# Five softmax normalisations of the first two token chunks on VectorE instead of GpSimd, one PSUM copy on ScalarE, and a new hand-written order

## The chip, the cores and the metric

The kernel runs on one core of one Trainium2 chip. The metric is the device time of one execution in microseconds (us). Engines are TensorE (PE in the profile; PEld are its weight loads), VectorE (DVE), ScalarE (ACT), GpSimd (POOL) and SyncE (SP), which issues the DMAs. Every engine runs its own queue in order; between queues the order is kept by semaphores.

## The reference

Sliding-window attention (window 64) over 8 batches, 8 heads, 576 positions and a head size of 64, followed by a two-layer network with a rational function between its layers. q, k, v and the output are float32; the two weight matrices arrive as float64.

```python
scores = (q @ k.T) / sqrt(64)                    # per batch and head
scores = where((rel >= 0) & (rel < 64), scores, -1e9)
attn = exp(scores - max(scores));  attn = attn / (sum(attn) + 1e-9)
x = (attn @ v) as [4608 tokens, 512]             # heads side by side
h = x @ w_in                                     # [4608, 2048]
P = a0 + a1*h + a2*h**2 + a3*h**3
Q = 1 + |b0|*|h| + |b1|*h**2
out = (P / (Q + 1e-6)) @ w_out                   # [4608, 512]
```

## The kernel before

**Work.** The 4608 tokens go in nine chunks c of 512. Each chunk has four *units* (c,hp), one for each pair of heads: SP loads q, k and v; TensorE makes the scores (L641; for the first two chunks a matmul with the mask, L624, comes first); VectorE takes the row maxima (L679, L680); ScalarE makes the exponentials and their sums (L691); VectorE inverts the sums (L698, L699); then *normalise* multiplies the probabilities `sm`, 128 x 1024, by the inverse (L703, on GpSimd); TensorE transposes them into two PSUM banks (L708); *copy_pT* brings them to SBUF (L716); TensorE multiplies by v into `ps_x` (*values*, L722); *x_high* rounds that to fp32r (L727) and *x_low* keeps the rest (L731, VectorE).

For each chunk there are then 16 steps over slices of 128 of the 2048 columns, 144 steps s in all. A step has *G* s (12 matmuls, L802: high and low parts of x and w_in), its rational function (ScalarE L808, L811, L814, L827, L830; VectorE L817 num1, L820 num2, L834 g_high, L838 product, L842 remainder, L847 g_low; GpSimd L824 u1) and *F* s.0 to s.3, one for each 128 tokens (3 matmuls each, L885, into four PSUM accumulators). Chunk 0 does its first 8 steps, then chunk 1 all 16, then chunk 0 the rest, and the other chunks follow.

The float64 weights come as 32 *tiles* of bits, W0i to W15i for w_in and W0o to W15o for w_out, and are taken apart once, within about the first 200 us: SP loads a tile (L501, L503), ScalarE scales its high words (L507 *scale*), GpSimd keeps the sign (L511 *sign*), VectorE joins the bits (L515 *put_sign*, L520 *put_low*), ScalarE makes the high part (L531 *high*) and VectorE the low one (L534 *rest*).

**PSUM.** `h` and `ps_x` share two buffers: a G or a unit's values wait until num2 or x_low has read the buffer's last owner. The scores of chunk 1 and all transposes share the two banks `b0` and `b1`.

**Order.** All of these operations go into a plan. A list scheduler gives each a start, but for the first 200 us a table `PLACE` (operation number to start) overrides it. The operations are emitted in the order of these starts, which sets the order of each engine's queue and nothing else; SP's DMAs wait for the buffer that they fill and block the DMAs behind them.

```python
for op in self.ops:
    op.start = PLACE.get(op.n, op.start)
return sorted(self.ops, key=lambda o: o.start)
```

Loads of w_st tiles stand in staging buffers of several pools: W0o and W4i, and the probabilities of unit (0,1), share the two `sm` buffers.

Of the kernel before, what the change touches and what calls it, by code (L numbers as in the profile page):

```python
# [13 lines left out]
ALU = mybir.AluOpType  # L14
# [31 lines left out]
class Plan:  # L46
# [25 lines left out]
    def order(self):  # L72
# [92 lines left out]
        for op in self.ops:  # L165
# [5 lines left out]
PLACE = {0: 8.17349, 1: 38.92356, 2: -5.9611, 3: 8.88229, 4: 1.33916, 5: 1.47189, 6: 3.78178, 7: 8.4872, 8: 9.67491,  # L171
# [123 lines left out]
def swa_rational_ffn(ctx: ExitStack, tc: tile.TileContext, qT, kT, v, w_in, w_out, a, b, out):  # L295
    nc = tc.nc
    P = 128
# [85 lines left out]
    wi_h, wi_l, wo_h, wo_l = {}, {}, {}, {}  # L383
# [36 lines left out]
    UN, GT, F2R, OUTR, N1, SG, LD = 0.3, 0.02, 0.5, -0.5, 0.0, 0, 2.0  # L420
    KEEP = 4
    PT_DVE = ((0, 0), (0, 1))
    XH_DVE = ((0, 0), (0, 1))
    LENT = ((0, 1),)
    MASK_US = 4.8
    PSC = 8
# [134 lines left out]
    def plan_unit(c, hp, rank):  # L561
# [12 lines left out]
        u = {}  # L574
# [415 lines left out]
```

## Time and profile before

| | |
|---|---|
| median of 3 runs | 956.92 us (956.54 to 958.22) |
| profiled execution, time | 956.61 us |
| profiled execution, span of instructions | 954.8 us |
| TensorE busy | 934.4 us, 98% of the span |
| VectorE busy | 789.6 us, 83% |
| ScalarE busy | 670.4 us, 70% |
| GpSimd busy | 331.0 us, 35% |
| mean granted clock of TensorE | 0.993 |

The busy shares are means over stages: a long steady stage of steps, and the first 200 us or so, in which weights are decoded too. The difference of 1.8 us between the profiled execution's time and its span lies around the instructions. In rows of the timeline the square bracket tells how long the engine idled before an instruction and what ended that.

### The profile page before, as it was taken

To read this page: it belongs to the slowest core of one execution; us is meant where nothing else is said; L and a number is where in the kernel's file an instruction comes from. 1 tells how busy PE (TensorE), PEld (TensorE's weight loads), DVE (VectorE), ACT (ScalarE), POOL (GpSimd) and SP (SyncE) were. 2 spreads that over 40 slices of the span, in tenths; PEclk is the share of its full clock that TensorE was granted. 3 is DMA by queue.
4 is the path that set the end of the run, shared out by engine and by line. 5 is a ranking of instruction groups with operands and counts; after the bars stand their busy time and mean duration, and the time that the engine had idled before them with its cause. 6 is when DMAs were issued, how large, how long until landed. Compare 5 with 4: busy or idle time off the path is not lost.

```text
span 954.8 us, 16307 instructions
## 1 busy us (share of the span) xinstructions
PE 934.4 (98%) x6068; PEld 751.6 (79%) x6068; DVE 789.6 (83%) x1198; ACT 670.4 (70%) x1477; POOL 331.0 (35%) x227
## 2 busy tenths in 40 slices
PE   7789999999999999999999999999999999999998
PEld 5567777878888888888888888888888888888886
DVE  5999999999797978887787787878879778777775
ACT  6787877778767676666767677667676676756564
POOL 5756456433423233232323233233132332322221
PEclk9899999999999999999999999999999999999999
DMA  8732315123421112101111121111211120001001
GB/s 317 244 133 65 131 46 154 46 92 104 136 82 44 44 44 87 44 13 58 61 44 44 43 81 50 45 48 48 92 46 46 46 83 31 1 1 45 0 1 45
DMA packets 39103, 66.47 MB, mean 70 GB/s; under 512 B 5616, under 2 KB 22256, under 8 KB 39024
## 3 DMA queue, kind: packets, MB, share of 16 engines
q1 hardware_dynamic: 39024, 65.43, 20.7%
q8 instruction: 48, 0.79, 0.3%
q14 instruction: 31, 0.25, 0.1%
HBM read 54.92 MB, written 10.49 MB: 69 GB/s over the span
## 4 chain that ended last, share of the span: by engine, by line
PE 88%; DVE 8%; ACT 2%; issue 1%; DMA 0%; POOL 0%; SPq 0%; ACTq 0%; DVEq 0%; POOLq 0%
PE o L885 39%; PE h L802 39%; PE ps_x L722 3%; PE banks L641 3%; PE banks L708 2%; ACT sm L691 1%; DVE gh L834 1%; DVE num L842 1%; DVE nmx L679 1%; DVE num L817 1%; DVE u L838 1%; DVE w_c L515 1%; DVE w_c L520 1%; DVE num L820 1%; DVE gl L847 1%
## 5 line engine op out<-in xcount | busy, mean ns | idle before, releaser
L824 POOL TENSOR_TENSOR u<-u,ah 128x512 f32<-128x512 f32 x144 | 204.7, 1422 | 417.6 <-ACT u L814 287.3
L802 PE MATMUL h<-xl,wi_h 128*128 128x512 f32 x576 | 230.3, 400 | 3.0 <-DVE num L820 2.4
L885 PE MATMUL o<-wo_h,gl 128*128 128x512 f32 x576 | 231.8, 402 | 0.1
L802 PE MATMUL h<-xh,wi_l 128*128 128x512 f32 x576 | 227.8, 395 | 0.0
L802 PE MATMUL h<-xh,wi_h 128*128 128x512 f32 x576 | 227.3, 395 | 0.0
L885 PE MATMUL o<-wo_h,gh 128*128 128x512 f32 x576 | 226.6, 393 | 0.0
L885 PE MATMUL o<-wo_l,gh 128*128 128x512 f32 x576 | 225.9, 392 | 0.0
L827 ACT ACTIVATE ah<-u 128x512 f32<-128x512 f32 x144 | 91.0, 633 | 118.7 <-POOL u L824 118.5
L834 DVE SCALAR_TENSOR_TENSOR gh<-num,a_sb,ah 128x512 fp32r<-128x512 f32 x144 | 109.1, 758 | 49.4 <-ACT ah L830 48.0
L808 ACT ACTIVATE ah<-h 128x512 f32<-128x512 f32 x144 | 85.9, 597 | 80.3 <-PE h L802 56.8
L817 DVE TENSOR_TENSOR num<-num,h 128x512 f32<-128x512 f32 x144 | 98.3, 683 | 45.6 <-ACT num L811 45.4
L802 PEld LDWEIGHTS h<-xl,wi_h 128*128 128x128 f32 x576 | 108.6, 189 | 32.4 <-DVE num L820 4.2
L885 PEld LDWEIGHTS o<-wo_h,gl 128*128 128x128 f32 x576 | 108.2, 188 | 26.3 <-issue 2.9
L802 PEld LDWEIGHTS h<-xh,wi_l 128*128 128x128 f32 x576 | 108.4, 188 | 26.0
L802 PEld LDWEIGHTS h<-xh,wi_h 128*128 128x128 f32 x576 | 108.5, 188 | 24.8
L885 PEld LDWEIGHTS o<-wo_h,gh 128*128 128x128 f32 x576 | 108.1, 188 | 25.2
L885 PEld LDWEIGHTS o<-wo_l,gh 128*128 128x128 f32 x576 | 108.3, 188 | 22.9 <-DVE wo_l L534 0.4
L703 POOL TENSOR_TENSOR sm<-sm,rs 128x1024 f32<-128x1024 f32 x36 | 70.1, 1948 | 151.2 <-ACT ah L808 87.6
L814 ACT ACTIVATE u<-ah,b_sb 128x512 f32<-128x512 f32 x144 | 117.2, 814 | 0.1
L842 DVE SCALAR_TENSOR_TENSOR num<-num,a_sb,u 128x512 f32<-128x512 f32 x144 | 114.9, 799 | 2.4
L838 DVE SCALAR_TENSOR_TENSOR u<-u,gh 128x512 f32<-128x512 f32 x144 | 105.8, 735 | 7.3 <-DVE gh L834 0.5
L811 ACT ACTIVATE num<-h,a_sb 128x512 f32<-128x512 f32 x144 | 111.7, 775 | 0.0
(80 smaller groups left out, 1095.4 us busy)
## 6 DMA issues: line engine op xcount, KB each, us to landing
out<-ob SPq DMA_DIRECT2D x35, 256.0 KB, 2.0
w_st<-w_in SPq DMA_DIRECT2D x16, 512.0 KB, 5.0
w_st<-w_out SPq DMA_DIRECT2D x16, 512.0 KB, 4.2
vt<-v SPq DMA_DIRECT2D x8, 448.0 KB, 6.1
vt<-v SPq DMA_DIRECT2D x8, 384.0 KB, 3.4
vt<-v SPq DMA_DIRECT2D x8, 320.0 KB, 3.6
q<-qT SPq DMA_DIRECT2D x8, 256.0 KB, 4.7
kt<-kT SPq DMA_DIRECT2D x8, 256.0 KB, 4.0
```

What stands on the lines that cost most here:

```text
L703: nc.gpsimd.tensor_tensor(out=sm, in0=sm, in1=u["rs"].unsqueeze(2).broadcast_to([P, NR, P]), op=ALU.mult)
L802: nc.tensor.matmul(h, w[i][:, cc, :], x[c, cc], start=n == 0, stop=n == 3 * NCC - 1)
L808: nc.scalar.activation(d["ah"], d["h"], AF.Abs)
L811: nc.scalar.activation(d["num"], d["h"], AF.Identity, scale=a_sb[:, 3:4], bias=a_sb[:, 2:3])
L814: nc.scalar.activation(d["u"], d["ah"], AF.Identity, scale=b_sb[:, 1:2], bias=b_sb[:, 0:1])
L817: nc.vector.tensor_tensor(out=d["num"], in0=d["num"], in1=d["h"], op=ALU.mult)
L824: nc.gpsimd.tensor_tensor(out=d["u"], in0=d["u"], in1=d["ah"], op=ALU.mult)
L827: nc.scalar.activation(d["ah"], d["u"], AF.Ln, bias=QADD)
L834: nc.vector.scalar_tensor_tensor(out=d["gh"], in0=d["num"], scalar=a_sb[:, 0:1], in1=d["ah"], op0=ALU.add, op1=ALU.mult)
L838: nc.vector.scalar_tensor_tensor(out=d["u"], in0=d["u"], scalar=QADD, in1=d["gh"].bitcast(F32), op0=ALU.add, op1=ALU.mult)
L842: nc.vector.scalar_tensor_tensor(out=d["num"], in0=d["num"], scalar=a_sb[:, 0:1], in1=d["u"], op0=ALU.add, op1=ALU.subtract)
L885: nc.tensor.matmul(acc[t], g[:, ts], w[i], start=first and n == 0, stop=last and n == 2)
```

## The change

Five units, (0,0), (0,3), (1,0), (1,1) and (1,3), get their normalise on VectorE; (0,1), (0,2) and (1,2) and all later chunks stay on GpSimd. x_high of (0,1) goes from VectorE to ScalarE ((0,0)'s stays on VectorE). In the last of the 144 steps the three matmuls of each F run in the order gh*wo_l, gh*wo_h, gl*wo_h in place of gl*wo_h, gh*wo_l, gh*wo_h. The table gets new starts for its 754 operations and 77 more.

```diff
-PLACE = {0: 8.17349, 1: 38.92356, ...
+PLACE = {...
...
     PT_DVE = ((0, 0), (0, 1))
-    XH_DVE = ((0, 0), (0, 1))
+    XH_DVE = ((0, 0),)
+    NORM_DVE = ((0, 0), (0, 3), (1, 0), (1, 1), (1, 3))
+    FIRST_TWO = (0, 0), (0, 1)
...
         def normalise():
             sm = u["sm"]
-            nc.gpsimd.tensor_tensor(out=sm, in0=sm, in1=u["rs"].unsqueeze(2).broadcast_to([P, NR, P]), op=ALU.mult)
+            (nc.vector if (c, hp) in NORM_DVE else nc.gpsimd).tensor_tensor(out=sm, in0=sm, in1=u["rs"].unsqueeze(2).broadcast_to([P, NR, P]), op=ALU.mult)
...
-            for n, (g, w) in enumerate(((d["gl"], wo_h), (d["gh"], wo_l), (d["gh"], wo_h))):
+            three = (d["gl"], wo_h), (d["gh"], wo_l), (d["gh"], wo_h)
+            for n, (g, w) in enumerate(three[1:] + three[:1] if s == total - 1 else three):
```

The scheduler's own costs are the same before and after (FIRST_TWO takes the place of the two other tuples there), so beyond the table the order is unchanged. What the new table does to the queues, where the prediction speaks of it:

- VectorE, before: (0,0) invert, (0,2) maxima, (0,1) invert, (0,0) copy_pT, (0,3) maxima, (0,2) invert, W0i put_sign, (0,1) copy_pT, (0,3) invert, W0i put_low, (0,0) x_high, x_low, (0,1) x_high, x_low, W0i rest, W1i put_sign, put_low, W2i put_sign, W1i rest, W2i put_low. After: (0,0) invert, **normalise**, (0,2) maxima, W0i put_sign, (0,1) invert, (0,0) copy_pT, (0,3) maxima, (0,2) invert, (0,0) x_high, (0,1) copy_pT, (0,0) x_low, W0i put_low, (0,3) invert, **normalise**, W0i rest, W1i put_sign, put_low, W2i put_sign, (0,1) x_low, W1i rest, W2i put_low.
- VectorE further on, after: (1,0) invert, **normalise**, G0 num1, (1,1) maxima, G0 num2 (before: invert, num1, num2, maxima); (1,1) invert, G0 g_low, **normalise**, G1 g_high, W6i rest; (1,3) maxima, G4 num1, (1,2) invert, G4 num2, G5 num1, G5 num2 (before: (1,2) invert, W3o put_low, G4 num1, (1,3) maxima, G4 num2, G5 num1, with G5 num2 four operations later); (1,3) invert, **normalise**, G4 g_high; and G6 num1 and num2 now ahead of (1,3) x_low.
- ScalarE: W0i scale now ahead of (0,1)'s exponentials and W2i scale ahead of (0,3)'s; x_high of (0,1) between (0,2) copy_pT and W3i scale.
- TensorE: (0,0) values ahead of (0,1) transposes; F0.0 ahead of (1,1) transposes, F1.0 ahead of (1,2) scores, and exchanges of neighbours of this kind up to 222 us.
- GpSimd: W0i sign, (0,1) normalise, W2i sign, (0,2) normalise, W1i sign, W3i sign.
- SP, before: q and k of (0,0), (0,1); W0i; q and k of (0,2); W2i; q and k of (1,1), (0,3); the two coefficient loads; W3i; v of (0,0); W1i; v of (0,1), (0,2), (0,3); W0o, W4i. After: q and k of (0,0), (0,2); the two coefficient loads; q and k of (0,1); v of (0,0); W0i, W1i; v of (0,2); q and k of (0,3); W2i, W4i; v of (0,1); q and k of (1,1); W0o, W3i; v of (0,3).

## Rows read from the trace of the kernel before

**Rows 1.** The page's head: the span, and busy time of the engines.

```profile
span 954.8 us, 16307 instructions
PE 934.4 (98%) x6068; PEld 751.6 (79%) x6068; DVE 789.6 (83%) x1198; ACT 670.4 (70%) x1477; POOL 331.0 (35%) x227
```

**Rows 2.** Table by stretches: the stretch and its length, busy us of each engine (instructions), granted clock, DMA share, GB/s.

```profile
40.00:50.00 10.00, 8.09 (x64) 6.03 (x62) 8.54 (x16) 10.00 (x36) 6.14 (x5) 1.00 0.91 344
90.00:100.00 10.00, 9.64 (x42) 7.51 (x41) 9.96 (x17) 6.73 (x12) 4.50 (x4) 1.00 0.31 112
130.00:140.00 10.00, 10.00 (x45) 8.06 (x44) 10.00 (x17) 7.77 (x13) 6.10 (x4) 1.00 0.04 12
240.00:300.00 60.00, 60.00 (x466) 48.62 (x465) 50.23 (x79) 44.37 (x104) 19.87 (x14) 1.00 0.26 87
```

**Rows 3.** Waits of TensorE from 36 to 205 us: who waited for whom, us in total, times, the longest.

```profile
PE h L802 <- DVE num L820: 2.4, 2, 1.6
PE bank L708 <- POOL u L824: 1.0, 1, 1.0
PE ps_x L722 <- DVE num L820: 0.7, 1, 0.7
PE bank L708 <- ACT sm L691: 0.7, 1, 0.7
PE h L802 <- DVE xl L731: 0.4, 1, 0.4
```

**Rows 4.** Timeline of VectorE: start and duration in us, instruction, and the idle time before it.

```profile
12.01 0.17 DVE L698 SCALAR_TENSOR_TENSOR sums<-sums,zero 128x8 f32<-128x8 f32 x1 [1.36 <-ACT sm L691]
13.59 1.29 DVE L679 TENSOR_REDUCE nmx<-ps_s 128x4 f32<-128x512 f32 x2 [1.18 <-PE ps_s L641]
...
17.15 1.29 DVE L679 TENSOR_REDUCE nmx<-ps_s 128x4 f32<-128x512 f32 x2 [0.60 <-PE ps_s L641]
...
21.94 0.17 DVE L698 SCALAR_TENSOR_TENSOR sums<-sums,zero 128x8 f32<-128x8 f32 x1 [0.89 <-ACT sm L691]
...
44.01 0.69 DVE L817 TENSOR_TENSOR num<-num,h 128x512 f32<-128x512 f32 x1 [1.27 <-ACT num L811]
...
53.93 2.39 DVE L534 SCALAR_TENSOR_TENSOR wi_l<-w_c,wi_h 128x512 fp32r<-128x512 f32 x1
...
76.37 1.38 DVE L680 SCALAR_TENSOR_TENSOR nmx<-nmx,zero 128x8 f32<-128x8 f32 x1
...
80.78 0.17 DVE L698 SCALAR_TENSOR_TENSOR sums<-sums,zero 128x8 f32<-128x8 f32 x1 [0.57 <-ACT sm L691]
82.34 1.71 DVE L834 SCALAR_TENSOR_TENSOR gh<-num,a_sb,ah 128x512 fp32r<-128x512 f32 x1
...
90.35 0.68 DVE L847 TENSOR_TENSOR gl<-num,ah 128x512 fp32r<-128x512 f32 x1
90.95 0.68 DVE L731 TENSOR_TENSOR xl<-ps_x,xh 128x512 fp32r<-128x512 f32 x1
```

**Rows 5.** Timeline of GpSimd: the normalise of (1,0), (1,1), (1,2) and (1,3).

```profile
42.91 1.90 POOL L703 TENSOR_TENSOR sm<-sm,rs 128x1024 f32<-128x1024 f32 x1 [2.74 <-ACT ah L808]
...
53.41 2.36 POOL L703 TENSOR_TENSOR sm<-sm,rs 128x1024 f32<-128x1024 f32 x1
...
75.83 1.89 POOL L703 TENSOR_TENSOR sm<-sm,rs 128x1024 f32<-128x1024 f32 x1
...
81.35 2.15 POOL L703 TENSOR_TENSOR sm<-sm,rs 128x1024 f32<-128x1024 f32 x1 [2.39 <-ACT ah L827]
```

**Rows 6.** Groups of VectorE's instructions by line and shape, whole span: busy us, mean ns of one, idle before.

```profile
L834 DVE SCALAR_TENSOR_TENSOR gh<-num,a_sb,ah 128x512 fp32r<-128x512 f32 x144 | 109.1, 758 | 49.4 <-ACT ah L830 48.0
L662 DVE SCALAR_TENSOR_TENSOR sm<-banks,mask 128x1024 f32<-128x1024 f32 x24 | 29.2, 1216 | 0.0
L671 DVE SCALAR_TENSOR_TENSOR sm<-banks,mask 128x256 f32<-128x256 f32 x20 | 8.3, 415 | 0.0
L534 DVE SCALAR_TENSOR_TENSOR wo_l<-w_c,wo_h 128x512 fp32r<-128x512 f32 x8 | 5.5, 681 | 0.0
L727 DVE CAST xh<-ps_x 128x512 fp32r<-128x512 f32 x2 | 1.4, 682 | 0.0
```

**Rows 7.** Timeline of TensorE and ScalarE ahead of G0: (0,3)'s values, the first matmul of G0, and W3i's scale on ScalarE.

```profile
31.75 2.45 PE L722 MATMUL ps_x<-pT,vt 128*64 128x64 f32 x32 [4.27 <-ACT pT L716]
37.20 0.59 PE L802 MATMUL h<-xl,wi_h 128*128 128x512 f32 x1
...
26.55 0.69 ACT L507 ACTIVATE w_c<-w_st 128x512 f32<-128x512 f32 x1 [0.76 <-DVE wi_l L534]
```

**Rows 8.** Table by stretches of the first 14 us, columns as in rows 2; the last one is GB/s of the DMAs.

```profile
0.00:8.00 8.00, 6.53 (x40) 3.25 (x40) 2.84 (x8) 1.58 (x2) 3.26 (x15) 1.00 0.76 257
8.00:12.00 4.00, 1.62 (x34) 1.05 (x33) 2.39 (x6) 2.93 (x17) 0.00 (x0) 1.00 1.01 379
12.00:14.00 2.00, 1.53 (x33) 1.05 (x33) 0.78 (x3) 2.00 (x13) 1.43 (x1) 1.00 0.79 91
```

**Rows 9.** Timeline of the last step: the last g_low, and the first matmul of the last step's F.

```profile
947.21 0.69 DVE L847 TENSOR_TENSOR gl<-num,ah 128x512 fp32r<-128x512 f32 x1
...
948.33 0.39 PE L885 MATMUL o<-wo_h,gl 128*128 128x512 f32 x1
```

**Rows 10.** Table by stretches, columns as in rows 2.

```profile
51.00:54.50 3.50, 3.50 (x11) 2.92 (x12) 3.47 (x7) 3.22 (x7) 2.85 (x2) 0.51 0.46 147
```

More of the change, by code (lines that the diff above doesn't have):

```diff
@@ L170 @@
 ENGINES = "PE", "DVE", "ACT", "POOL", "SP"
-PLACE = {0: 8.17349, 1: 38.92356, 2: -5.9611, 3: 8.88229, 4: 1.33916, 5: 1.47189, 6: 3.78178, 7: 8.4872, 8: 9.67491,
[111 rows of a table removed]
+PLACE = {0: 2.76379, 1: 30.07498, 2: 0.33636, 3: 4.34826, 4: 4.11576, 5: 4.27481, 6: 6.83819, 7: 9.75642, 8:
[123 rows of a table added]
 class Early:
@@ L756, in plan_unit @@
         o = link("transposes", plan.add("PE", 0.872, r(7), transposes, [o, chain.get("transposes")], [ssm] + spt, kind="T"))
-        o = plan.add("DVE" if (c, hp) in PT_DVE else "ACT", 1.0 if joined else 1.3 if (c, hp) in PT_DVE else 1.1, r(8), copy_pT, [o],
+        o = plan.add("DVE" if (c, hp) in FIRST_TWO else "ACT", 1.0 if joined else 1.3 if (c, hp) in FIRST_TWO else 1.1, r(8), copy_pT, [o],
                      spt + [spT])
@@ L764, in plan_unit @@
         link("values", o)
-        oh = plan.add("DVE" if (c, hp) in XH_DVE else "ACT", 0.69 if (c, hp) in XH_DVE else 0.594, r(10), x_high, [o] + free_x.get(c, []), [spx])
+        oh = plan.add("DVE" if (c, hp) in FIRST_TWO else "ACT", 0.69 if (c, hp) in FIRST_TWO else 0.594, r(10), x_high, [o] + free_x.get(c, []), [spx])
         o = plan.add("DVE", 0.688, r(11), x_low, [oh], [spx])
```

234 rows, old and new, of the table PLACE are left out of this document.

## The prediction

> **What bounds the kernel now.** The page comes first: TensorE is busy for 98% of the span [rows 1]. So the end is TensorE's last matmul plus a short tail, and a change can only move the end by the time that TensorE loses. The table by stretches says where that is [rows 2]: from 240 us on TensorE is busy all of the time and VectorE 84% of it (50.2 of 60 us); from 90 to 200 us VectorE is at 10 of 10 us too, and ahead of that TensorE has holes. The waits of TensorE from 36 to 205 us [rows 3] name VectorE: `h` and `ps_x` (one pair of PSUM buffers) wait for L820 or L731, which read the buffer last. Before G0 (the first gate products, at 37.20) TensorE idles 4.27 us for unit (0,3)'s pT copy [rows 7]; that copy stands in ScalarE's queue behind weight tiles that wait for VectorE. From 92 to 200 us VectorE has no hole and TensorE hardly one: the two keep step, so what VectorE is early or late at about 92 us passes to TensorE, and after 240 us nothing gives it back. The last wait of the stage is G7's, for unit (1,3)'s x_low, which ends at 90.95 + 0.68 = 91.63 [rows 3, 4]. I therefore price the change on VectorE's queue between unit (0,0)'s invert (12.01) and that x_low.
>
> What VectorE loses there, idle or stretched [rows 4]: idle 1.18 (13.59), 0.60 (17.15), 0.89 (21.94), 1.27 (44.01), 0.57 (80.78); stretched L534 at 53.93 by 2.39 - 0.68 = 1.71, L680 at 76.37 by 1.38 - 0.17 = 1.21 (0.17 is what L698, as small, takes at 12.01), L834 at 82.34 by 1.71 - 0.76 = 0.95 [rows 4, 6]. Sum 8.38 us. Smaller stretches beside GpSimd's other operations I leave as they are. The three long ones lie under a GpSimd normalise each and end a little over 0.5 us after it [rows 4, 5]: the one of 53.41 ends at 55.77, and L534, which takes 0.68, ends at 56.32. An operation with a PSUM input is not held: L817 at 44.01 takes 0.69 under the normalise of 42.91.
>
> The Trainium skill (SBUF — State Buffer, "SBUF: two separate sides") says that GpSimd and a VectorE operation with two SBUF inputs exclude each other for a whole instruction; these rows agree. The Trainium skill (Perfetto Trace Analysis, "Optimizing Scalar/DVE Operations") advises the reverse of this change, to move work off a saturated VectorE, to GpSimd if need be, and adds that between those two it may not help because of the shared port; what the advice would make of it here is the rival "VectorE pays" below.
>
> **The change, part by part.**
>
> *Five normalises on VectorE.* No row has this operation there. By the slope of L662 (1024 elements, 1.216) and L671 (256, 0.415) an element costs 1.04 ns; L534 with two SBUF inputs takes 0.681 for 512, so 0.681 + 0.53 = 1.21 us [rows 6]. Back to back, operations start some 0.07 before the one ahead ends (90.95 is 0.60 after the operation ahead of it, which lasts 0.68), so I take 1.15, 5.75 for five. Lower bound 1.13; upper bound GpSimd's own 1.90 [rows 5], 9.5 for five; the rows of VectorE itself are nearest.
>
> *x_high of (0,1) to ScalarE:* VectorE -0.68 [rows 6]. ScalarE does it in about as much in a stretch in which it waited for VectorE before (0.76 idle at 26.55 [rows 7]), so nothing; without that cover, 0.7 in the queue ahead of (0,3)'s copy. Net work added to VectorE: 5.75 - 0.68 = 5.07 us.
>
> *What goes in exchange.* (0,0): its normalise fits the idle 1.18 ahead of (0,2)'s maxima, which wait for scores: 1.18 back, and the transposes come 0.75 earlier. (0,3) and the new order to 24 us: W0i's put_sign stands ahead of (0,1)'s invert, and its scale runs on ScalarE ahead of (0,1)'s exponentials; walked through with the durations of before, VectorE has no hole from 12 to 22 us, 1.4 of 1.49 back. GpSimd, freed of two normalises, reaches the signs of W1i and W2i earlier. (1,0): its normalise falls into the 1.27 in which VectorE waits for ScalarE's L811: 1.15 back. (1,1): the 1.71 under GpSimd's normalise goes. (1,3): the 0.95 goes, and of the 0.57 ahead of its invert 0.4. (1,2) stays on GpSimd, but its invert now comes after (1,3)'s maxima, and the next three operations on VectorE (num2, num1, num2 of G4 and G5) read PSUM: 1.0 of 1.21 back. Sum 7.8. New waits: W3i's load is now queued behind w_out 0, which waits for (0,1)'s transposes, and its sign may hold VectorE: -0.4. So VectorE is at G6.num2 or x_low, where G7 gets its buffer, 7.8 - 5.07 - 0.4 = 2.3 us sooner.
>
> *Can TensorE follow?* It idles 2.4 us at G2 and G6 together, 1.0 and 0.7 at (1,0)'s transposes and 0.7 at (1,0)'s values, in all 4.8 [rows 3], beside the hole before G0. G0 should come about 1.7 us earlier, the rest at G6 and (1,0)'s values. (1,1)'s maxima move ahead of G0.num2, which makes G2 later by the 1.3 us that they last; the cover is that (1,0)'s transposes wait for (1,1)'s exponentials to leave the banks anyway; were that gone, 1.3 us are lost.
>
> *Clock.* TensorE runs at the lower of its two levels, 1.2 of 2.4 GHz (0.51 granted), from 51 to 54.5 us [rows 10], after the waits at G2 and at (1,0)'s transposes; 3.5 us then do the work of 1.75. Shorter holes could spare some of it, new ones bring another: +-1.7 us, 0 taken.
>
> *SP's queue.* (0,2)'s q and k and the two coefficient loads pass (0,1)'s q and k; w_in 0 moves behind (0,0)'s v, w_in 3 and (0,3)'s v far back, w_in 1, w_in 4 and w_out 0 forward. Up to w_in 0 the queue now holds 2.5 MB; before, 2.06 MB had moved by 8 us and 379 GB/s followed, so its bytes are in at about 9.2 us [rows 8]. ScalarE wants it at 11.9, when (0,0)'s sums are done [rows 4]. The fall to 91 GB/s at 12 to 14 us, behind the coefficient loads, should go. Taken as 0; bound: each us that w_in 0 lands after 11.9 delays the exponentials of the next unit by as much.
>
> *Last step's order (gl last).* The first matmul of the last step starts at 948.33; gl is ready at 947.21 + 0.69 = 947.90 [rows 9]. TensorE does not wait, so 0; if gl came later by over 0.43 us, up to two matmuls (0.46) would be won.
>
> *After 92 us* the work on all engines is the same and only reordered: 0, with +-0.8 for new or lost small holes.
>
> **Sum.** 956.61 (profiled execution: span 954.8 and 1.8 around it) - 2.3 = 954.3; its own time is 0.3 under the median of the runs, 956.92, so on the median's scale 954.6. I give 954.5.
>
> **Rivals.**
> *VectorE pays.* Place: x_low of (1,3) and G7. VectorE is full from 92 to 200 us and TensorE hangs on it, so each us added before is a us at the end. If only the two stretches under moved normalises (1.71 + 0.95) come back and the holes stay because ScalarE or PSUM sets them, the price is 5.07 - 2.66 = +2.4: 959.3. It decides for slower where less than 3.2 of the 8.38 comes back. Against it: the idle at 13.59 and 44.01 lies exactly where normalises go. Chance 0.12. This is the time by the advice on a saturated VectorE as well.
> *Nothing comes through.* The early ScalarE queue or a late load (w_in 0, w_in 3, (0,3)'s v) keeps (0,3)'s copy near 31 us, or the 5.07 eats what is won: 3.84 from (0,0), (1,1), (1,3) and a third of the other 4.54, 5.4 in all, against 5.07 and the 0.4 of new waits. For it: ScalarE is full from 40 to 50 us (10.0 of 10) [rows 2]. 956.9. Chance 0.31.
> *More than that.* All 8.38 back, G0 some 3.5 us earlier and half of the half clock spared: 8.38 - 5.07 + 0.9 = 4.2: 952.7. The hole of 4.27 us before G0 speaks for it, TensorE's own work against. Chance 0.15.
> Forecast 0.42, with its own range of 953.3 to 956.
>
> **Numbers.** A measurement here tells no less than 0.2%, 1.9 us, from no change. Faster by more: 0.15 and nearly all of 0.42, and a little of the second rival: 0.55. Within: 0.33. Slower: 0.12. Range: down to 951.8, the third rival with the other half of the clock's loss, up to 958.4, between the second rival and the first; what is left out is a tenth on either side at most.
>
> **What the profile after would show.** L703 on VectorE, five times, near 1.2 us; the one of (0,0) starting at 12.4 and its transposes before 14; no L534 of 2.4 near 53 and no L834 of 1.7 near 82; the idle ahead of L817 near 44 gone; G0 at 35 to 36; G7 at 89 to 90; VectorE still full from 90 to 200; last matmul near 949. The forecast is wrong if L703 on VectorE takes much over 1.3, if ScalarE waits for w_in 0 near 12 or VectorE for W3i's sign near 27, or if TensorE's holes reappear behind another wait.

## The result, and the profile after

The kernel got slower: 962.87 us (median of 6 runs, 961.81 to 963.64) against 956.73 (6 runs beside them), a ratio of 1.0061 (95% interval 1.0048 to 1.0074). The prediction, 954.5 us and faster (range 951.8 to 958.4), was wrong. The head of the page of the changed kernel, which answers to [rows 1]: the profiled execution took 962.08 us, its span is 5.5 us longer than before, TensorE's busy time is the same within 0.4 us (934.4 before), and VectorE is busy 5.5 us more (789.6 before), about what the five normalises less the copy were said to add.

```profile
span 960.3 us, 16310 instructions
PE 934.8 (97%) x6068; PEld 751.1 (78%) x6068; DVE 795.1 (83%) x1202; ACT 671.2 (70%) x1478; POOL 320.7 (33%) x222
```

So TensorE does the same work with 5 us more of waiting. The start of several operations in both traces, in us, shows where the waiting arose (the difference to before in the last column):

| operation | before | after | later by |
|---|---|---|---|
| maxima of (0,1), VectorE | 9.16 | 12.96 | 3.80 |
| normalise of (0,0) | 12.57 | 14.80 | 2.23 |
| G0, TensorE | 37.20 | 38.72 | 1.52 |
| G7 | 91.69 | 94.63 | 2.94 |
| G12 | 118.17 | 120.59 | 2.42 |
| G18 | 151.67 | 155.57 | 3.90 |
| G26 | 195.52 | 201.57 | 6.05 |
| exponentials of (2,3), ScalarE | 234.34 | 239.73 | 5.39 |

Some 2.4 us are lost ahead of 118 us and, by the last row, another 3 behind it. (At G26 the difference is larger, because the new order also puts other work ahead of that gate.) The prediction had 2.3 us won ahead of 92 us and nothing behind.

**The start.** First the DMA rates of the first 16 us, in 40 slices of 0.4 us: the upper line is the busy share in tenths, the lower GB/s.

```profile
DMA  0000599999995911123788899999999999999999
GB/s 0 0 0 0 108 189 333 364 348 277 358 302 166 109 31 46 32 47 124 272 310 324 339 395 382 454 411 406 440 413 421 421 399 416 399 406 437 415 416 430
```

From 4.8 to 7.6 us the engines move 31 to 166 GB/s. That is the same hole which [rows 8] have at 12 to 14 us (91 GB/s): it has moved forward with the coefficient loads, which are now ahead of the queries and keys of (0,1) and of W0i. TensorE waits for those keys (timeline of TensorE; the time in brackets is its idle time and what ended it), VectorE for TensorE, and ScalarE for W0i (timelines of VectorE and of ScalarE):

```profile
11.38 1.57 PE L655 MATMUL ps_s<-kt,q 64*64 64x128 f32 x32 [4.02 <-DMA kt<-kT]
```

```profile
12.96 1.29 DVE L693 TENSOR_REDUCE nmx<-ps_s 128x4 f32<-128x512 f32 x2 [4.72 <-PE ps_s L655]
...
14.37 0.16 DVE L712 SCALAR_TENSOR_TENSOR sums<-sums,zero 128x8 f32<-128x8 f32 x1
14.56 0.20 DVE L713 RECIPROCAL rs<-sums 128x8 f32<-128x8 f32 x1
14.80 1.32 DVE L717 TENSOR_TENSOR sm<-sm,rs 128x1024 f32<-128x1024 f32 x1
```

```profile
13.62 0.66 ACT L521 ACTIVATE w_c<-w_st 128x512 f32<-128x512 f32 x1 [2.37 <-DMA w_st<-w_in]
14.55 0.37 ACT L705 ACTIVATE sm<-ps_s,nmx 128x128 f32<-128x128 f32 x1 [0.27 <-DVE sums L712]
```

The invert of (0,0) (L712) had its sums near 11.3, but stands behind the maxima of (0,1) in VectorE's queue, and these wait for the keys; so the normalise that was to start at 12.4 starts at 14.80. The wait for W0i is the one that the prediction named as its own refutation.

**Waits of TensorE from 36 to 205 us**, answering to [rows 3]:

```profile
PE h L816 <- DVE num L834: 3.6, 2, 2.4
PE ps_x L736 <- DVE num L834: 2.2, 1, 2.2
PE o L900 <- DVE gl L861: 2.1, 3, 1.2
PE o L900 <- ACT ob L912: 1.3, 1, 1.3
```

The first two are those of before and grew (2.4 and 0.7); (1,0)'s transposes no longer wait. The last two are new, and lie in output products (L900), which before had no wait to show here. Little of it is the lower clock: the granted clock from 40 to 62 us is 0.92 in both.

**Near 126 us**, the wait for `ob` (the copy of an output product on its way to memory), in the timelines of TensorE, ScalarE and SP's queue:

```profile
126.21 0.51 PE L900 MATMUL o<-wo_h,gl 128*128 128x512 f32 x1 [1.27 <-ACT ob L912]
```

```profile
125.01 0.64 ACT L521 ACTIVATE bank<-w_st 128x512 f32<-128x512 f32 x1 [1.64 <-DMA w_st<-w_out]
125.58 0.58 ACT L912 COPY ob<-o 128x512 f32<-128x512 f32 x1
```

```profile
112.91 0.33 SPq L917 DMA_DIRECT2D part<-ob  x1
113.80 0.80 SPq L515 DMA_DIRECT2D w_st<-w_in  x2
116.84 0.33 SPq L917 DMA_DIRECT2D part<-ob  x1
117.36 0.33 SPq L515 DMA_DIRECT2D w_st<-w_in  x1
120.77 0.33 SPq L517 DMA_DIRECT2D w_st<-w_out  x1
```

Read from below: W9o's load is issued at 120.77, when the second spilled part (116.84) has landed; SP waits 3.0 us for that. That part shares the DMAs with the loads of W11i and W13i (113.80). Before, W11i came much earlier, W13i behind W9o, and W9o's load went out at 116.73. W9o lands at 125.0; its scaling is at the head of ScalarE's queue, behind it is the copy that TensorE waits for. This is the table's new late order, with no normalise in it.

**Near 179 us**, timelines of VectorE, GpSimd and TensorE:

```profile
177.56 1.66 DVE L861 TENSOR_TENSOR gl<-num,ah 128x512 fp32r<-128x512 f32 x1
```

```profile
177.36 1.32 POOL L838 TENSOR_TENSOR u<-u,ah 128x512 f32<-128x512 f32 x1 [0.24 <-ACT u L828]
```

```profile
179.37 0.47 PE L900 MATMUL o<-wo_h,gl 128*128 128x512 f32 x1 [0.59 <-DVE gl L861]
```

In the kernel before, the same operation (timeline of VectorE):

```profile
172.93 0.69 DVE L847 TENSOR_TENSOR gl<-num,ah 128x512 fp32r<-128x512 f32 x1
```

G19's g_low, which took 0.69 before, now lies under G20's product on GpSimd (177.36 to 178.68) and ends 0.54 us behind it: the held VectorE operation of the prediction, at a new place.

### The profile page after: what moved, and what is told of

It is laid out like the page before. It is cut to its first block, busy times and chain, and to the rows that moved or that the text cites. A ratio compares the mean times of both kernels' runs of the same rounds, so it can differ in the third digit from the quotient of the medians.

```text
span 960.3 us, 16310 instructions
## 1 busy us (share of the span) xinstructions
PE 934.8 (97%) x6068; PEld 751.1 (78%) x6068; DVE 795.1 (83%) x1202; ACT 671.2 (70%) x1478; POOL 320.7 (33%) x222
## 4 chain that ended last, share of the span: by engine, by line
PE 81%; DVE 1%; ACT 0%; issue 0%; ACTq 0%
PE o L900 36%; PE h L816 36%; PE ps_x L736 3%; PE banks L655 3%; PE banks L722 2%; PE bank L655 0%; PE bank L722 0%; DVE gl L861 0%; ACT ah L841 0%; DVE u L852 0%; DVE num L856 0%; ACT u L828 0%; ACT num L825 0%; DVE wo_l L548 0%; DVE gh L848 0%
## 5 line engine op out<-in xcount | busy, mean ns | idle before, releaser
L900 PE MATMUL o<-wo_h,gl 128*128 128x512 f32 x576 | 232.1, 403 | 3.4 <-DVE gl L861 2.1
L900 PE MATMUL o<-wo_h,gh 128*128 128x512 f32 x576 | 226.6, 393 | 0.0
L900 PE MATMUL o<-wo_l,gh 128*128 128x512 f32 x576 | 225.9, 392 | 0.0
L900 PEld LDWEIGHTS o<-wo_h,gl 128*128 128x128 f32 x576 | 108.2, 188 | 30.6 <-issue 3.7
L900 PEld LDWEIGHTS o<-wo_h,gh 128*128 128x128 f32 x576 | 108.1, 188 | 25.2
L900 PEld LDWEIGHTS o<-wo_l,gh 128*128 128x128 f32 x576 | 108.3, 188 | 22.6
L834 DVE SCALAR_TENSOR_TENSOR num<-num,a_sb,h 128x512 f32<-128x512 f32 x144 | 107.1, 744 | 2.4
```

What stands on the lines that cost most here:

```text
L834: nc.vector.scalar_tensor_tensor(out=d["num"], in0=d["num"], scalar=a_sb[:, 1:2], in1=d["h"], op0=ALU.add, op1=ALU.mult)
L900: nc.tensor.matmul(acc[t], g[:, ts], w[i], start=first and n == 0, stop=last and n == 2)
```

## Experiments

Each is compared with runs of the kernel before on the same chip (956.6 to 956.8 us); the ratio is to those, with its 95% interval. What is edited is mostly the table: `PLACE[n]` orders operation n on its engine, and a diff like `-0: 2.76379` is one entry of it (0: the coefficient loads, 15 and 28: the queries and keys of (0,1) and (0,2), 103: W0i's scaling, 256 and 284: the loads of W11i and W13i, 331: G0.num2). Each diff is against the kernel named in the sentence ahead of it. In the experiments' rows the line numbers are one or two lower than in the changed kernel.

**The two halves.** The table of the changed kernel for what starts by 95 us in the table of before, the rest from before (h_early); and the opposite (h_late). In words, for the tables are long:

```diff
-PLACE = table of the changed kernel
+PLACE = operations under 95.0 in the table of before: in the changed order, below 95.0; all others: table of before
```

> The changed kernel whose table is cut at about 95 us: the operations that the kernel before starts by 95 us stand in the changed kernel's order, all later ones in the order of before; the engines are the changed kernel's. Late-order theory (about half of the loss arises behind 95 us, from the new order there): the shift of 2.3 to 2.5 us that the trace of the changed kernel has at 100 us stays to the end and nothing is added, some 959.2 us, 1.0025 of before. Start theory (the coefficient loads early in SP's queue cost it all, and the rest follows from that) and VectorE-pays theory (five normalises at 1.25 us): both lie wholly ahead of 95 us, so all of it stays, some 962.8 us, 1.006.

```diff
-PLACE = table of the changed kernel
+PLACE = operations under 95.0 in the changed table: in the order of before, below 95.0; all others: changed table
-    XH_DVE = ((0, 0),)
-    NORM_DVE = ((0, 0), (0, 3), (1, 0), (1, 1), (1, 3))
+    XH_DVE = ((0, 0), (0, 1))
+    NORM_DVE = ()
```

> The opposite cut: what the changed kernel starts by 95 us stands in the order of before, with the engines of before (GpSimd normalises all units, VectorE has its copy back); all later ones stand in the changed kernel's order, the last step's product order too. Late-order theory: slower than before by the 2.5 to 3.5 us that the changed kernel's shift grows by behind 100 us, 959 to 960 us, with W9o's load landing late near 125 us again. Start theory and VectorE-pays theory: no change from before, 956.7 us within 0.2%.

h_early: 960.18 us, 1.0037 (1.0024 to 1.0049). h_late: 959.50, 1.0034 (1.0021 to 1.0046). By medians +3.6 and +2.9 us, together 6.5 against the 6.1 of the whole. The loss has two parts of similar size that add up, and the later one needs no normalise on VectorE.

**The coefficient loads**, in the changed kernel behind W2i's load (a_coef), and in the kernel before second in the queue (b_coef2):

```diff
-0: 2.76379
+0: 13.94523
```

> The changed kernel with one move: the two coefficient loads go from third in SP's queue to behind W2i's load. Start theory: the hole in the transfers at 5 to 8 us goes, the keys of unit (0,1) land 2.5 to 4 us sooner, ScalarE's wait of 2.37 us for W0i shrinks, and the end comes 1.5 to 2.7 us sooner, 960 to 961.4 us; if all of the loss comes from there, 957. VectorE-pays and late-order theories: within 0.5 us of the changed kernel, 962.4 to 963.4 us.

```diff
-0: 8.17349
+0: -5.42119
```

> The kernel before with one move: the two coefficient loads go from eighth in SP's queue to second, ahead of unit (0,1)'s queries and keys. Start theory: the hole in the transfers comes at 4 to 7 us in place of 12 to 14, unit (0,1) and W0i land 2.5 to 4 us later, and the end comes 1.5 to 2.7 us later, 958.2 to 959.4 us. The two other theories: no change, 956.7 us within 0.5 us.

a_coef: 959.17 us, 1.0029 (1.0017 to 1.0040): 3.5 of the 6.1 us are gone with one line of the table. (0,1)'s maxima start at 9.95, W0i is there when ScalarE wants it (11.51), G0 starts at 34.37, 2.8 us ahead of before. b_coef2: 957.02, 1.0006 (0.9997 to 1.0015): 0.4 us by the medians and not told from nothing, where 1.5 to 2.7 were expected, although the hole is there, its (0,1)'s maxima start at 11.29 and its profiled execution (its slowest, 958.46) is 1.9 us late at G26. The hole alone is not yet the loss.

**How late the keys of (0,1) are.** In the changed kernel these loads alone go ahead (a_u01); then W0i's scaling behind the exponentials of (0,1) as well (e_w0i, against a_u01). And the kernel before gets the start of the changed queue (e_b_sp):

```diff
-15: 2.76398
+15: 1.12766
```

> The changed kernel (962.87 us) with one move: the queries and keys of unit (0,1) go from fourth in SP's queue to second, ahead of those of (0,2) and of the coefficient loads; these stay ahead of W0i's load. Theory that the late keys of (0,1) are what the early coefficient loads cost: the maxima of (0,1) start near 9.5 in place of 12.96 us and the end comes 2.5 to 3.7 us sooner, 959.2 to 960.4 us, as with the loads moved. Theory that W0i's late landing does it, with ScalarE waiting for it ahead of the exponentials of (0,1): W0i lands as late as before, ScalarE waits longer, and the end stays at 962.3 to 963.4 us.

```diff
-103: 11.16352
+103: 15.19724
```

> The changed kernel with the queries and keys of unit (0,1) second in SP's queue (960.46 us) and one move more: on ScalarE the scaling of W0i goes behind the exponentials of (0,1). The coefficient loads stay ahead of W0i's load. Theory that the rest of what the early coefficient loads cost (1.3 us, from 960.46 down to the 959.17 us of the kernel with the loads moved) is the wait for W0i at the head of ScalarE's queue: the exponentials of (0,1) start near 12 in place of 13.36 us and the end comes 0.8 to 1.5 us sooner, 959.0 to 959.7 us. Rival (the rest is the hole in the transfers itself, whose later loads all land later): 960.5 us within 0.6.

```diff
-0: 8.17349
-28: 7.43977
+0: -4.88228
+28: -4.88328
```

> The kernel before whose SP queue starts as the changed kernel's: the queries and keys of (0,0), those of (0,2), the two coefficient loads, then those of (0,1) and W0i's load; every engine keeps the order of before, with the scaling of W0i behind the exponentials of (0,1). Theory that the late keys of (0,1) cost as much in either order: 2.0 to 3.0 us slower than before, 958.6 to 959.8 us. Theory that the order of before has the room for it (with the loads second in its queue it lost 0.4 us): 0.3 to 1.2 us slower, 956.9 to 957.8 us.

a_u01: 960.46 us, 1.0043 (1.0030 to 1.0056), 2.4 us less than the changed kernel by the medians (the two intervals just overlap): the keys look like the larger part. e_b_sp: 959.82, 1.0035 (1.0023 to 1.0047), with (0,1)'s maxima at 13.30: the start of the changed queue costs the order of before 3.1 us, as much as it costs the changed one. So the room that one theory gave the order of before does not exist. What b_coef2 lacks is the second pair of loads, (0,2)'s, ahead of (0,1). (0,2)'s loads alone in that place were not tried in the order of before; in a_coef, where they stand there without the coefficient loads, the maxima start at 9.95. So it seems to take the two together to make the keys this late.

e_w0i missed: 962.36 us, 1.0053 (1.0041 to 1.0066), where one theory had 959.0 to 959.7 and the other 960.5. The exponentials of (0,1) did start sooner, at 11.70 in place of 13.36. But VectorE's queue has W0i's put_sign ahead of the invert of (0,1), put_sign needs GpSimd's sign, and the sign needs the scaling, which the edit itself had moved from 12.78 to 14.44 (timelines of ScalarE, GpSimd and VectorE in e_w0i):

```profile
14.44 0.77 ACT L520 ACTIVATE w_c<-w_st 128x512 f32<-128x512 f32 x1
15.29 1.56 POOL L524 TENSOR_SCALAR w_st<-w_st 128x512 f32<-128x512 f32 x1 [10.95 <-ACT w_c L520]
```

```profile
16.89 0.69 DVE L528 SCALAR_TENSOR_TENSOR w_c<-w_c,w_st 128x512 uint32<-128x512 uint32 x1 [1.92 <-POOL w_st L524]
17.50 0.16 DVE L711 SCALAR_TENSOR_TENSOR sums<-sums,zero 128x8 f32<-128x8 f32 x1
```

At 14.44 the scaling waited for no load any more: this wait was made by the edit, not by W0i. In a_u01 put_sign starts at 15.14 and the invert at 16.28, so a lead of 1.7 us had become a loss of 1.2. The edit moved the wait from one queue to another, and the share of W0i's late landing is therefore not separated from that of the hole.

**W9o's load.** On a_coef, the loads of W11i (256) and W13i (284) go behind it (c_w9o):

```diff
-256: 115.66375
-284: 117.10621
+256: 119.86306
+284: 121.02547
```

> The changed kernel with the coefficient loads behind W2i's load (959.17 us) and one move more: the loads of W11i and W13i go from ahead of the second spilled part of the seventh output product to behind W9o's load. Late-load theory: W9o's load, which waited on SP for that part's transfer and landed near 122 to 125 us with ScalarE and then VectorE waiting, lands 2 to 4 us sooner, the hole of TensorE near 123 to 126 us (1.3 to 1.8 us) goes, and the end comes 1.0 to 1.8 us sooner, 957.4 to 958.2 us. Rival (the late loss is spread over the new order and the hole was only where it shows): 959.2 us within 0.6.

957.75 us, 1.0016 (1.0007 to 1.0025), 1.4 us less than a_coef by the medians, as expected; the two intervals overlap, but the wait itself is gone. ScalarE no longer waits for W9o and TensorE is full from 120 to 130 us (8.73 us busy in the changed kernel; timeline of ScalarE, table by stretches of c_w9o, columns as in [rows 2]):

```profile
120.08 0.63 ACT L520 ACTIVATE bank<-w_st 128x512 f32<-128x512 f32 x1
120.63 0.59 ACT L911 COPY ob<-o 128x512 f32<-128x512 f32 x1
```

```profile
120.00:130.00 10.00, 10.00 (x45) 8.03 (x44) 9.93 (x16) 7.70 (x14) 5.37 (x4) 1.00 0.33 117
```

**Both taken out.** a_coef's table up to 95 us and before's behind it (c_early_coef); c_w9o's table up to 165 us and before's behind it (d_best); both against the changed kernel.

```diff
-PLACE = table of the changed kernel
+PLACE = operations under 95.0 in the table of before: in the order of a_coef, below 95.0; all others: table of before
```

> The changed kernel with both found causes taken out: the coefficient loads behind W2i's load, and behind 95 us the order of the kernel before. VectorE still normalises the five units. Theory of two causes (the coefficient loads in the early part, the new order in the late part; nothing else): the trace of the changed kernel with the loads moved stands between 1.3 us sooner and 1.0 us later than before at 92 to 106 us, so the end is that of before within 1 us, 955.5 to 957.5 us. VectorE-pays theory (five normalises at 1.25 us, less the copy, cost VectorE 5 us that only partly come back): still 2.4 us slower, 959 us.

```diff
-PLACE = table of the changed kernel
+PLACE = operations under 165.0 in the table of before: in the order of c_w9o, below 165.0; all others: table of before
```

> The changed kernel with the coefficient loads behind W2i's load, the loads of W11i and W13i behind W9o's, and the order of the kernel before from 165 us on (957.75 us with the changed kernel's order there). Theory of a third place (from 170 us on the new order puts the high part of W12o and the scaling of W13o ahead of the nineteenth gate step's chain, and TensorE stands 0.6 us at 177 us): the end comes 0.8 to 2 us sooner than with the changed order, 955.6 to 957.0 us; and if the lead of 1.6 us that this kernel's trace had on before at 163 us is kept, it ends ahead of before, near 955.5. Rival (the late order is harmless there and the lead is one execution's chance): 957.7 us within 0.6.

c_early_coef: 956.97 us, 1.0007 (0.9998 to 1.0016): no longer told from before, with all five normalises on VectorE. d_best: 957.34, 1.0004 (0.9995 to 1.0013). Against c_w9o that is 0.4 us by the medians and 1.2 by the ratios, less than their intervals, so the times alone do not prove the third place, near 179 us. The traces do. Counted by the starts of the matmuls of G and F, each of the seven traces with the changed order there (changed kernel, a_coef, a_u01, e_w0i, h_late, c_w9o, c_normG) falls 1.4 to 1.5 us further behind before between the matmuls that before starts at 167 and at 181 us, those of d_best and d_num2 0.4 and all others nothing, and what was lost there is still lost at 250 us. The lead of 1.6 us at 163 us was one execution's chance: d_best's own trace, of the same order up to there, is 0.3 us behind before at G20.

**What the normalise itself is worth.** c_normG is a_coef with the engine put back, b_norm5 the kernel before with that engine change alone:

```diff
-    NORM_DVE = ((0, 0), (0, 3), (1, 0), (1, 1), (1, 3))
+    NORM_DVE = ()
```

> The changed kernel with the coefficient loads behind W2i's load (959.17 us), and GpSimd normalises all units again, in the changed kernel's order. The prediction's step (a normalise on VectorE shortens each unit's path by 0.4 to 1.7 us): slower by 1 to 3 us, 960 to 962 us. VectorE-pays theory (VectorE has no idle time between 12 and 62 us, so its 6.2 us of normalises are paid): faster by 1 to 3 us, 956 to 958 us. Both hold and cancel: 959.2 us within 0.6.

```diff
+    NORM_DVE = ((0, 0), (0, 3), (1, 0), (1, 1), (1, 3))
...
-            nc.gpsimd.tensor_tensor(out=sm, in0=sm, in1=u["rs"].unsqueeze(2).broadcast_to([P, NR, P]), op=ALU.mult)
+            (nc.vector if (c, hp) in NORM_DVE else nc.gpsimd).tensor_tensor(out=sm, in0=sm, in1=u["rs"].unsqueeze(2).broadcast_to([P, NR, P]), op=ALU.mult)
```

> The kernel before with the engine of the five normalises changed and nothing else: VectorE in place of GpSimd, in the table of before; the copy of unit (0,1) stays on VectorE. The prediction's step: the paths of (1,0), (1,1) and (1,3) get 0.7 to 1.1 us shorter each, and 1 to 2 us of it reach the end, 954.7 to 955.8 us. VectorE-pays theory: 1.0 to 2.4 us slower, 957.7 to 959.1 us. Both hold and cancel: 956.7 us within 0.6.

c_normG: 960.51 us, 1.0044 (1.0031 to 1.0058), 1.3 us slower than a_coef by the medians. The two intervals overlap, but only one of a_coef's runs (960.38) reaches the fastest of c_normG (960.26): in the new order it is likely that VectorE's normalises do pay. b_norm5: 956.33, 0.9999 (0.9990 to 1.0008): in the order of before gain and price cancel. The theory that VectorE pays them in full fails both times.

**G2's buffer, and the last step.** d_num2 is d_best with G0.num2 back ahead of (1,1)'s maxima on VectorE; b_tail is the kernel before with the last step's order alone.

```diff
-331: 32.3096
+331: 32.03016
```

> The kernel of the line before this with one move more: on VectorE the second product of gate step 0's numerator goes back ahead of the maxima of unit (1,1), where it stood in the kernel before. Order theory (the lead of 2.8 us that the first gate step has in the start is lost because TensorE waits 2.9 us for this product to free a buffer): the third gate step starts 1.0 to 1.5 us sooner and 0.5 to 1.4 us reach the end. Theory that VectorE is full from 12 to 62 us: the third gate step starts sooner, but the exponentials of (1,1) 0.7 us later, and the end moves by less than 0.4 us.

```diff
-            for n, (g, w) in enumerate(((d["gl"], wo_h), (d["gh"], wo_l), (d["gh"], wo_h))):
+            three = (d["gl"], wo_h), (d["gh"], wo_l), (d["gh"], wo_h)
+            for n, (g, w) in enumerate(three[1:] + three[:1] if s == total - 1 else three):
```

> The kernel before with the last step's three products in the changed order and nothing else. The prediction's step (no effect): 956.6 us within 0.4. Rival (the product that waits for the low part of the gate no longer stands first, so the last step ends sooner): 0.5 to 0.7 us sooner, 955.9 to 956.1 us.

d_num2: 956.58 us, 1.0001 (0.9993 to 1.0010). G2 starts at 43.84 in place of 46.39, 2.5 us sooner; at F0.1 0.5 us of it are left, at G4 none (66.45 against 66.22). VectorE's queue had only 1.3 us of lead to give (G2's num2 at 56.50 in place of 57.80), TensorE waited the longer for it, and then ran (1,0)'s values, among others, at the lower clock: 0.50 granted from 58 to 60 us, 1.00 in d_best (timelines of TensorE in d_num2 and in d_best):

```profile
57.30 1.92 PE L735 MATMUL ps_x<-pT,vt 128*64 128x64 f32 x32 [3.00 <-DVE num L833]
```

```profile
58.60 1.15 PE L735 MATMUL ps_x<-pT,vt 128*64 128x64 f32 x32 [1.67 <-DVE num L833]
```

b_tail: 956.61, 1.0000 (0.9991 to 1.0009): nothing. No version of these beats the kernel before by more than a measurement can tell.

## Why the prediction was wrong, point by point

**SP's queue, taken as 0, is the step that failed most.** It names the loads that pass (0,1)'s queries and keys and then prices W0i alone, by bytes: in at 9.2 us. The bytes were no guide, since the hole of [rows 8] belongs to the two coefficient loads and moves with them; W0i was waited for until 13.6. And the first unit to suffer was (0,1), whose keys TensorE waited for until 11.38, a transfer that the step gave no due time at all. Even the sentence on the hole ("should go") was there; where it would go was not asked. Price: 3.5 us (a_coef). How much of it is the late keys and how much W0i is known by the medians only (a_u01: 2.4 and the rest). The bound, that each us that W0i lands late delays the exponentials by as much, held in a_u01 (W0i's scaling at 12.78, the exponentials at 13.36).

**"After 92 us: 0 +- 0.8" failed second.** h_late shows 2.9 us, of which 1.4 are W9o's load (c_w9o) and, by the traces, about as much the held g_low near 179 us. The work is the same and only reordered, but a reordered queue of loads is not nothing: the step did not look at which load had moved past which spill, nor at what GpSimd would hold.

**The exchange on VectorE (7.8 back, 5.07 paid, 2.3 us sooner at G7) was too good.** Freed of the hole, a_coef stands 0.4 us behind before at G7 (the four traces of its start lie at 91.43 to 92.56, three of before's order, before, b_norm5 and b_tail, at 90.88 to 91.71), and c_early_coef ends level with it. The engine change alone is worth 1.3 us by the medians in the new order and nothing in the old. The terms: a normalise lasts 1.22 to 1.32 us and once 1.68 (1.21 said); the idle times ahead of (0,2)'s maxima and L817 went, as said. But the stretches under GpSimd went elsewhere (timelines of VectorE and of GpSimd in a_coef):

```profile
20.95 1.48 DVE L533 SCALAR_TENSOR_TENSOR w_c<-w_st,w_c 128x512 uint32<-128x512 uint32 x1
...
52.08 1.68 DVE L716 TENSOR_TENSOR sm<-sm,rs 128x1024 f32<-128x1024 f32 x1
...
54.94 1.76 DVE L851 SCALAR_TENSOR_TENSOR u<-u,gh 128x512 f32<-128x512 f32 x1
...
75.13 1.22 DVE L693 SCALAR_TENSOR_TENSOR nmx<-nmx,zero 128x8 f32<-128x8 f32 x1
```

```profile
19.99 1.90 POOL L716 TENSOR_TENSOR sm<-sm,rs 128x1024 f32<-128x1024 f32 x1
...
51.79 1.81 POOL L524 TENSOR_SCALAR w_st<-w_st 128x512 f32<-128x512 f32 x1 [3.71 <-ACT w_c L520]
54.61 1.54 POOL L837 TENSOR_TENSOR u<-u,ah 128x512 f32<-128x512 f32 x1 [1.01 <-ACT u L827]
...
73.74 2.59 POOL L837 TENSOR_TENSOR u<-u,ah 128x512 f32<-128x512 f32 x2 [5.75 <-ACT u L827]
```

0.8 us more than the 0.68 of its kind for W0i's put_low, 0.45 for (1,1)'s normalise, 1.07 for G1's product: 2.3 us of new stretches, as much as the whole forecast gain. And the 1.21 at the maxima, of which 1.0 was to come back, stayed 1.22 in full length: GpSimd's gate products hold it now. Added up for VectorE from (0,0)'s invert to 92 us, the stretches (those over 0.15 us, against the shortest operation of the kind) fall from 6.9 us in before to 5.7 in a_coef and the idle time from 4.7 to 0.8. So 5.1 us came back, not 7.8: the idle part of the sum (4.1) was right, the stretched part (3.7) gave 1.2. I counted each stretch as tied to the normalise that caused it and did not ask what GpSimd, coming earlier, would hold next. The Trainium skill (SBUF — State Buffer, "SBUF: two separate sides") has GpSimd and such a VectorE operation exclude each other for the whole instruction, whichever of GpSimd's reads SBUF. The rows of 20.95 and 54.94 agree, ending 0.54 and 0.55 us after GpSimd's; the normalise of 52.08 takes only 0.45 longer and ends 0.16 us after, which is less than a whole instruction's wait.

The three terms together, 3.5, 2.9 and the 2.3 not won, make 8.7 us against the 8.4 between 954.5 and 962.87.

**"Can TensorE follow?"** G0 came as early as said and more in a_coef (34.37), but G2 waited for G0.num2 behind (1,1)'s maxima: the 1.3 us that the step named and called covered. TensorE stood 2.93 us there (timeline of TensorE in a_coef). d_num2 shows that taking this away does not reach the end either: from 40 to 62 us VectorE is busy 21.7 of 22 us in a_coef and 21.3 in d_num2, and what lead was left went in the next wait and the lower clock behind it.

```profile
45.92 0.50 PE L815 MATMUL h<-xl,wi_h 128*128 128x512 f32 x1 [2.93 <-DVE num L833]
```

**Right were** the last step's order (0; b_tail), the new engine's price per normalise within 0.1 us (four of the five), the clock taken as 0 (0.92 from 40 to 62 us in both), and that VectorE and TensorE keep step from 92 us on: what was late there stayed late to the end. The copy on ScalarE was not tried by itself. The rivals: "VectorE pays" (959.3) had the sign and not the cause; "nothing comes through" named a late W0i as a mechanism and let it only eat the gain (956.9), where it and the keys cost 3.5 us beyond that.

## What to carry to other kernels

When a queue of transfers is reordered, give every transfer that is passed a due time from the trace and ask of each one moved what it did to its successors where it stood before: a slow small load takes its hole along. Check each late stretch that is "only reordered" for a load that has passed another or a spill, and name the engine at whose queue's head its first reader stands. A stall by an excluded engine is not always removed by moving the operation under which it was seen; it lies under whatever that engine does at that time. The same five normalises took 3.1 us of stretches away in b_norm5's order and 1.2 in a_coef's.

## What the runs showed of the hardware

The two coefficient loads move almost nothing (128 partitions of 16 and of 8 bytes), yet a stretch of 2.0 to 3.2 us at under 200 GB/s moves with them: 12.0 to 14.4 us in before, 4.8 to 7.6 in the changed kernel, 7.2 to 9.2 in a_u01 (down to 1 GB/s), and in b_coef2, where they are second in the queue, 3.6 to 6.8 us (same view as above). In a_coef, with nothing else moved, it is gone from 4.8 to 7.6; the rate there is 220 to 358 GB/s. The view of b_coef2:

```profile
DMA  0000839992190241589999999999999999999899
GB/s 0 0 0 0 72 82 364 394 344 60 16 31 21 52 21 52 195 338 389 420 399 415 374 415 415 425 420 441 332 369 405 403 406 373 389 350 452 332 378 271
```

They land 6.5 and 6.9 us after they are issued in the changed kernel. Why such small transfers stop the queue's others was not tried. And the same order does not give the same start twice: a_coef, c_w9o, c_early_coef and d_best, alike up to 95 us, start G3 at 51.17, 51.68, 52.30 and 52.31 us, and the kernel before and b_tail, alike up to the last step, start G0 at 37.20 and 35.89. So a lead of one trace under some 1.3 us says little.
